# Finer rings for the streamed weights of the token MLP, later ordering of SP's tasks and tighter scheduling margins in a fused attention and MLP kernel

## The chip, the cores and the metric

One core of one Trainium2 chip. The metric is the device time of one execution in microseconds (us), the median of several executions. Spans and granted clocks belong to single executions; the granted TensorE clock was 0.999 to 1.000 in every profiled run here.

## The reference

With x of 2048 tokens by 1024, xn its layer norm, 32 heads, 4 segments of 512 tokens, the kernel computes

```python
xn = layernorm(x)
A: q, k, v = xn@wq, xn@wk, xn@wv              # per segment: causal softmax(q k^T) v, gated with a
   o = g * (phi(q) M) / (phi(q) z) + (1-g) * softmax(..) v   # memory M, z summed over earlier segments
   A = o @ wo
B: h = layernorm(xn)
   u = gelu(h^T-mixed: einsum('sd,sf->df', h, w1) + b1)       # w1: 2048 x 3584, mixes tokens
   B = (einsum('df,fs->ds', u, w2) + b2)^T                    # w2: 3584 x 2048
out = x + A + B
```

The first 215 us are the first MLP product. After that TensorE alternates between attention and the "dense" second product: 32 groups (16 token blocks by two halves), each the sum over 28 row blocks of w2 (for most groups plus 8 matmuls of `o @ wo`). Dense groups fill the time in which attention waits for ACT, POOL or DVE. w2 isn't resident; it is streamed through small rings.

## The kernel before

A Python scheduler inside the kernel keeps a model of every engine's time and decides in which order instructions are written. All DMAs are issued by SP, in program order; a DMA whose wait isn't met holds up all behind it (in the profile before, SP's queue spends 337 us waiting for PE).

```python
class _Ring:                                   # pieces of w2
    def ensure(self, b):
        target = min(b + self.depth, len(self.srcs) - 1)
        while self.issued <= target:           # load piece b+depth when piece b is first used
            k = self.issued
            src, dst = self.srcs[k], self.slots[k % self.n]
            self.fw.dma(dst[:, 0:src.shape[1], :], src, writes=[self.res[k % self.n]])
            self.issued += 1
# ...
class _Flow:
    MARGIN = 120          # a PE task is taken when its inputs are ready this many ns (by the model) ago
    MARGIN_STEP = 110
    PART = 160
    def next(self):                            # which waiting ACT/DVE/POOL/SP task is written next
        # ...
            for e, (fn, ns, busy) in t.engs.items():
                s = max(r, fw.now[e])
                key = (s, t.prio, t.n, s + ns)
# ...
        self.w2r = [e.take(f"w2n{i}", [P, 6, P], BF16) for i in range(4)]   # ring N: 4 pieces of 6
        self.w2l = [e.take(f"w2l{i}", [P, 6, P], BF16) for i in range(3)]   # ring L: 3 pieces of 6
# ...
        self.L = _Stream(k, self, long, "L", k.w2l, k.R_w2l, 2, [3])        # depth 2
        self.N = _Stream(k, self, rest, "N", k.w2r, k.R_w2, 3, [0, 1, 2])   # depth 3
# ... the end of tail(): last projection, by pieces of the last four token blocks
                fw.op("dve", lambda e: e.tensor_tensor(dst, self.ps[:, b, c0:c1], dst, op=ALU.add), ...)
                fw.dma(self.out_d[:, 4 * s + i, h * 512 + c0:h * 512 + c1], dst, ..., is_output=True)
```

The softmax here doesn't subtract the row's maximum and nothing guards it: scores larger than these inputs give would overflow.

Of the kernel before, what the change touches and what calls it, by code (L numbers as in the profile page):

```python
# [6 lines left out]
ACT = mybir.ActivationFunctionType  # L7
ALU = mybir.AluOpType
BF16 = mybir.dt.bfloat16
# [9 lines left out]
P = 128  # L19
# [346 lines left out]
class _Flow:  # L366


    LOOK = 5
    MARGIN = 120  # L370
    MARGIN_STEP = 110
    PART = 160

    def __init__(self, fw, R_bank, free, fill):
        self.fw, self.R_bank, self.free, self.fill = fw, R_bank, free, fill
# [59 lines left out]
    def next(self):  # L435
        fw, best = self.fw, None
        for t in self.avail:
            if t.gate is not None and not t.gate():
                continue
            reads = t.reads if t.box is None else t.reads + [self.R_bank[t.box["b"]]]  # L440
            r = fw.ready(reads, t.writes)
            for e, (fn, ns, busy) in t.engs.items():
                s = max(r, fw.now[e])
                key = (s, t.prio, t.n, s + ns)
                if best is None or key < best[0]:
                    best = (key, t, e, reads)
        return best
# [63 lines left out]
    def run(self, goals):  # L511
# [5 lines left out]
        while self.crit:  # L517
# [3 lines left out]
            for t in self.crit[:self.LOOK]:  # L521
                if t.wall and t is not self.crit[0]:
                    break
                if t.left == 0:
                    r = fw.ready(t.reads, t.writes)
                    if len(self.free) >= t.banks and not (t.wall and not fill.ready(t)):
                        bs = sorted(self.bank_t(b) for b in self.free)[:t.banks]
                        r = max([r, bs[-1]] if t.parts is None else [r, bs[3], bs[-1] - self.PART])
                        if r + (self.MARGIN_STEP if t.wall else self.MARGIN) <= now:
                            pick = t  # L530
# [53 lines left out]
class _Kernel:  # L584
# [95 lines left out]
    def over_early(self):  # L680
        fw = self.fw
        e = _Arena(self.nc, self.early_base, self.early_end)
        wait = _after(*self.R_xin, *self.R_xnt)
        self.wv_sb = e.take("wv_sb", [P, N_DCH, D_MODEL], BF16)
        self.wqr = [e.take(f"wq{i}", [P, N_DCH, P], BF16) for i in range(2)]
        self.wkr = [e.take(f"wk{i}", [P, N_DCH, P], BF16) for i in range(2)]
        self.w2r = [e.take(f"w2n{i}", [P, 6, P], BF16) for i in range(4)]
        self.w2l = [e.take(f"w2l{i}", [P, 6, P], BF16) for i in range(3)]
        self.w2s = [e.take(f"w2s{i}", [P, P], BF16) for i in range(2)]
        self.prod = e.take("prod", [P, 4, P], BF16)  # L690
        self.R_prod = Res("prod", wait)
        self.o_s = [e.take(f"o_s{i}", [P, 4, P], BF16) for i in range(2)]
        self.R_os = [Res(f"o_s{i}", wait) for i in range(2)]
        self.R_wv = [Res(f"wv{i}", wait) for i in range(2)]
        self.R_wq = [Res(f"wq{i}", wait) for i in range(2)]
        self.R_wk = [Res(f"wk{i}", wait) for i in range(2)]
        self.R_w2 = [Res(f"w2n{i}", wait) for i in range(4)]
        self.R_w2l = [Res(f"w2l{i}", wait) for i in range(3)]
        self.R_w2s = [Res(f"w2s{i}", wait) for i in range(2)]
        self.pkT = e.take("pkT", [P, SEG_L], BF16)  # L700
        self.etmp = e.take("etmp", [P, SEG_L], BF16)
        self.R_pkT = Res("pkT", wait)
        self.R_etmp = Res("etmp", wait)
        self.wq_ring = _Ring(fw, [t[:] for t in self.wqr], self.R_wq)
        self.wk_ring = _Ring(fw, [t[:] for t in self.wkr], self.R_wk)
        for i in range(N_UNIT):
            g = i % N_GRP
            self.wq_ring.srcs.append(self.A_wq[:, g * P:(g + 1) * P].rearrange("(dc p) j -> p dc j", p=P))
            self.wk_ring.srcs.append(self.A_wk[:, g * P:(g + 1) * P].rearrange("(dc p) j -> p dc j", p=P))
        self.fill = _Fill(self)  # L710
        self.wq_ring.ensure(0)
        self.wk_ring.ensure(0)
        for bv in range(2):
            fw.dma(self.wv_sb[:, :, bv * 512:(bv + 1) * 512],
                   self.A_wv[:, bv * 512:(bv + 1) * 512].rearrange("(dc p) j -> p dc j", p=P), writes=[self.R_wv[bv]])
# [311 lines left out]
        return self.flow.pe(mms, [R_w] + self.R_xnT[4 * s:4 * s + 4])[0]  # L1027

    def evac(self, dst, R_dst, box, view=lambda x: x):
        self.flow.op({"act": (lambda e, b: e.activation(dst, view(self.bank(b)), ACT.Copy), 600, 540),  # L1030
                      "dve": (lambda e, b: e.tensor_copy(dst, view(self.bank(b))), 690, 727)},  # L1031
                     [], [R_dst], box=box, give=True, prio=0)

# [68 lines left out]
    def step(self, items):  # L1102
        fl = self.flow
        slots, jobs, reads = [], [], []
        for r, blocks in items:
            slot = self.slots.popleft()
            slots.append(slot)
            col, masks = 0, []
            for u, kb in blocks:
                self.slot_of[u, r, kb] = (slot, col)  # L1110
                jobs.append((len(slots) - 1, u, r, kb, col))
                masks.append(col // P)
                col += SEG_L - kb * P
                for R in (self.R_kT[u % 3], self.R_qT[u % 3]):
                    if R not in reads:
                        reads.append(R)
            self.users[slot] = {u for u, _ in blocks}
            items[len(slots) - 1] = (r, blocks, slot, masks)

        n = fl.stage - 1  # L1120
        rs = (3 - n) % 4
        fill = self.fill

        def mms(bs, some):
            for i, u, r, kb, col in some:
                self.fw.mm(self.ps[:, bs[i], col:col + SEG_L - kb * P],
                           self.kT[u % 3][32 * r:32 * r + 32, kb * P:(kb + 1) * P],
                           self.qT[u % 3][32 * r:32 * r + 32, kb * P:SEG_L],
                           start=True, stop=True, tile_position=(32 * r, 0))

        def second(bs, some):
            if n >= fill.PLAIN and fill.L.sliced():
                fill.L.cut(rs)
            mms(bs, some)

        def parts(bs):
            k = min(4, len(bs))
            one = sorted([j for j in jobs if j[0] < k], key=lambda j: j[4])
            two = sorted([j for j in jobs if j[0] >= k], key=lambda j: j[4])
            r1 = [R for R in reads if R is not None]  # L1140
            res = [(lambda: mms(bs, one), r1, bs[:k], 330)]
            if two:
                res.append((lambda: second(bs, two), r1 + (fill.L.slice_reads() if n >= fill.PLAIN else []), bs[k:], 307))
            return res

        box = fl.pe(None, reads, banks=len(slots), wall=True, parts=parts)
        pT, R = self.pT, self.R_pT
        for i, (r, blocks, slot, masks) in enumerate(items):
            fl.op({"act": (lambda e, b, slot=slot: e.activation(pT[:, slot, :], self.bank(b), ACT.Exp, scale=SCALE),  # L1149
                           620, 488)}, [], [R[slot]], box=box[i], give=True)  # L1150
            v = pT[:, slot, :].rearrange("p (j q) -> p j q", q=P)
            if len(masks) > 1:
                ap, pat = v[:, masks[0]:masks[1] + 1:masks[1] - masks[0], :], [[0, 2], [1, P]]
            else:
                ap, pat = v[:, masks[0], :], [[1, P]]
            ns = 180 + 115 * len(masks)
            fl.op({"pool": (lambda e, ap=ap, pat=pat: e.affine_select(ap, ap, pattern=pat, compare_op=ALU.is_ge,  # L1157
                                                                      fill=0.0, base=0, channel_multiplier=-1),
                            ns, ns + 30)}, [R[slot]], [R[slot]])
# [99 lines left out]
    def attention_and_out(self):  # L1259
        fw = self.fw  # L1260
# [15 lines left out]
        steps = self.logit_steps()  # L1276
# [27 lines left out]
                    break  # L1304
        goals = [0, 0]
        knots = [(0, 0)] + [(last[8 * s + 7] + 2, 216 + 285 * s) for s in range(3)]
        knots += [(len(steps) - 1, self.fill.total - self.RESERVE), (len(steps), self.fill.total - 3)]
        for i in range(1, len(steps) + 1):
            (x0, y0), (x1, y1) = next((k0, k1) for k0, k1 in zip(knots, knots[1:]) if k0[0] <= i <= k1[0])
            goals.append(y0 + (y1 - y0) * (i - x0) / (x1 - x0))  # L1310
# [162 lines left out]
class _Fill:  # L1473
# [4 lines left out]
    def __init__(self, k):  # L1478
        self.k = k
        self.closed = []  # L1480
        rest = [(c, half, False, 0) for c in range(12, 16) for half in range(2)]
        long = []
        for j in range(3):
            g = [(c, half, True) for c in range(4 * j, 4 * j + 4) for half in range(2)]
            long += [x + (1,) for x in g[:3]]
            rest += [x + (0,) for x in g[3:]]
        long[-1] = long[-1][:3] + (0,)
        self.L = _Stream(k, self, long, "L", k.w2l, k.R_w2l, 2, [3])
        self.N = _Stream(k, self, rest, "N", k.w2r, k.R_w2, 3, [0, 1, 2])
        self.streams = [self.L, self.N]  # L1490
        self.total = self.L.total() + self.N.total()

# [107 lines left out]
```

## Time and profile before

| | before |
|---|---|
| median of 3 | 692.19 us (691.87 to 692.76) |
| span of the profiled execution | 690.2 us |
| PE busy / weight loads busy | 680.5 / 328.6 us |
| PE idle in waits (drawn) | 3.1 us: 1.3 start, 1.1 fixed gaps, 0.4 w2n, 0.3 mask |
| w2n loads, w2l loads | 115, 45 |
| long transposing issues on SP (over 1.4 us) | 4 of 56 after 200 us |

```profile
q8 instruction: 38, 0.62, 0.4%
q14 instruction: 16, 0.13, 0.1%
```

### The profile page before, as it was taken

The page shows a single profiled execution, that of the slowest core. Times are in us where ns is not written, and L with a number is a line of the kernel's source. Part 1 is how long each engine was busy: PE and PEld are TensorE (multiplying, and loading weights), DVE is VectorE, ACT ScalarE, POOL GpSimd, SP SyncE. Part 2 cuts the span into 40 slices and gives each one's busy share as a digit, 9 for nine tenths or more (in the row PEclk, how much of TensorE's full clock was granted, in tenths as well). Part 3 has the DMA queues.
Part 4 walks back from the last instruction along what each step waited for, and adds up shares of the span by engine and source line. Part 5 has one row for each costly group of instructions (what it writes and reads, how often), then busy time and mean ns, then how long its engine had stood idle before and what let it go on. Part 6 is the DMA issues. An engine that isn't in the chain of part 4 may idle for free.

```text
span 690.2 us, 11956 instructions
## 1 busy us (share of the span) xinstructions
PE 680.5 (99%) x4765; PEld 328.6 (48%) x4846; DVE 226.8 (33%) x500; ACT 313.5 (45%) x616; POOL 153.2 (22%) x379
## 2 busy tenths in 40 slices
PE   9999999999999999999999999999999999999998
PEld 3444444444444544544454444544545544454544
DVE  6731100000002323333453461633534534341524
ACT  7431111111136566564655462735754643644540
POOL 5820000000001233223223131312331331312330
PEclk9999999999999999999999999999999999999999
DMA  8367666325026558766556556465565456446334
GB/s 307 121 183 181 154 156 211 91 61 145 1 103 154 133 135 167 142 142 154 132 121 145 123 123 150 103 151 121 126 149 114 104 119 159 106 111 127 86 85 137
DMA packets 274960, 92.03 MB, mean 133 GB/s; under 512 B 233434, under 2 KB 271322, under 8 KB 274906
## 3 DMA queue, kind: packets, MB, share of 16 engines
q1 hardware_dynamic: 274906, 91.28, 54.1%
q8 instruction: 38, 0.62, 0.4%
q14 instruction: 16, 0.13, 0.1%
HBM read 74.47 MB, written 5.24 MB: 115 GB/s over the span
## 4 chain that ended last, share of the span: by engine, by line
PE 96%; issue 1%; ACT 1%; DMA 1%; POOL 0%; DVE 0%; SPq 0%; POOLq 0%; DVEq 0%
PE ps_all L217 96%; DMA xin<-in_A_x_dram 0%; DMA w2n<-in_B_w_dram 0%; ACT xn_tmp L851 0%; ACT xn_tmp L849 0%; POOL pT L1157 0%; DVE h L890 0%; POOL ln_r L882 0%; ACT pT L1149 0%; SPq L247 0%; DVE qT L1031 0%; POOLq L580 0%; DVE fin L1343 0%; POOL ln_t L880 0%; POOL ln_t L877 0%
## 5 line engine op out<-in xcount | busy, mean ns | idle before, releaser
L1157 POOL TENSOR_SCALAR_AFFINE_SELECT pT<-pT 128x256 bf16<-128x256 bf16 (+1 forms) x320 | 127.0, 405 | 506.8 <-ACT pT L1149 497.1
L217 PE MATMUL ps_all<-h,w1all 128*128 128x512 bf16 x878 | 192.9, 379 | 1.1
L1149 ACT ACTIVATE pT<-ps_all 128x512 bf16<-128x512 f32 x320 | 162.1, 620 | 48.9 <-PE ps_all L217 48.9
L217 PE MATMUL ps_all<-gT,w2n 128*128 128x512 bf16 x618 | 146.8, 379 | 2.2 <-issue 0.5
L217 PEld LDWEIGHTS ps_all<-h,w1all 128*128 128x128 bf16 x896 | 87.5, 98 | 106.3 <-DVE h L890 0.6
L1004 ACT ACTIVATE gT<-ps_all,bc 128x512 bf16<-128x512 f32 x56 | 37.7, 689 | 140.3 <-PE ps_all L217 134.8
L217 PEld LDWEIGHTS ps_all<-gT,w2n 128*128 128x128 bf16 x644 | 60.0, 98 | 69.6 <-issue 2.9
L1200 ACT ACTIVATE ost<-ps_all 128x264 bf16<-128x264 f32 (+1 forms) x99 | 35.0, 375 | 81.8 <-PE ps_all L217 81.0
L217 PE MATMUL ps_all<-xnT,wk 128*128 128x512 bf16 x255 | 60.4, 379 | 0.1
L1463 DVE SCALAR_TENSOR_TENSOR stg<-ps_all,bc,stg 128x512 bf16<-128x512 f32 x32 | 23.9, 747 | 110.7 <-PE ps_all L217 110.6
L217 PE MATMUL ps_all<-wv_sb,xnT 128*128 128x512 bf16 x254 | 59.9, 379 | 0.1
L217 PE MATMUL ps_all<-xnT,wq 128*128 128x512 bf16 x248 | 58.9, 379 | 0.4
L217 PE MATMUL ps_all<-gT,w2l 128*128 128x512 bf16 x226 | 57.8, 380 | 1.1 <-issue 0.5
L217 PEld LDWEIGHTS ps_all<-vA,pT 128*128 128x128 bf16 x1280 | 44.3, 96 | 14.2 <-POOL pT L1157 0.8
L1030 ACT ACTIVATE kT<-ps_all 128x512 bf16<-128x512 f32 x32 | 19.1, 597 | 60.6 <-PE ps_all L217 60.5
L217 PE MATMUL ps_all<-vA,pT 128*128 128x33 bf16 x1280 | 45.0, 177 | 0.5 <-POOL pT L1157 0.3
L217 PEld LDWEIGHTS ps_all<-wv_sb,xnT 128*128 128x128 bf16 x256 | 25.1, 98 | 30.2
L217 PEld LDWEIGHTS ps_all<-xnT,wk 128*128 128x128 bf16 x256 | 25.1, 98 | 30.2
L942 DVE TENSOR_SCALAR gcol<-gcol 128x32 f32<-128x32 f32 x1 | 0.2, 181 | 118.6 <-ACT gcol L940 118.6
L217 PEld LDWEIGHTS ps_all<-xnT,wq 128*128 128x128 bf16 x256 | 24.8, 98 | 29.0 <-issue 0.3
L217 PEld LDWEIGHTS ps_all<-gT,w2l 128*128 128x128 bf16 x244 | 21.3, 98 | 25.1 <-issue 5.8
L1015 DVE TENSOR_SCALAR etmp<-etmp 128x512 bf16<-128x512 bf16 x48 | 14.1, 293 | 55.1 <-ACT etmp L1014 55.1
(74 smaller groups left out, 489.2 us busy)
## 6 DMA issues: line engine op xcount, KB each, us to landing
w2n<-in_B_w_dram SPq DMA_DIRECT2D x92, 192.0 KB, 2.8
w1all<-in_B_w_dram SPq DMA_DIRECT2D x12, 1024.0 KB, 5.3
wq<-in_A_wq_dram SPq DMA_DIRECT2D x32, 256.0 KB, 2.8
wk<-in_A_wk_dram SPq DMA_DIRECT2D x32, 256.0 KB, 3.2
w2l<-in_B_w_dram SPq DMA_DIRECT2D x36, 192.0 KB, 2.9
stg<-in_A_x_dram SPq DMA_DIRECT2D x32, 128.0 KB, 3.3
out_dram<-stg SPq DMA_DIRECT2D x32, 128.0 KB, 2.0
w2n<-in_B_w_dram SPq DMA_DIRECT2D x23, 128.0 KB, 2.5
```

Source lines behind the costliest of these rows:

```text
L217: ins = self.nc.tensor.matmul(out, *args, **kwargs)
L942: fw.op("dve", lambda e: e.tensor_scalar(self.gcol[:], self.gcol[:], 1.0, None, op0=ALU.add), reads=[self.R_gcol], writes=[self.R_gcol])
L1004: fw.op("act", lambda e: e.activation(self.gT[:, fc, half * 512:(half + 1) * 512], self.bank(b), ACT.Gelu_apprx_tanh, bias=self.b1c[:, fc: ...
L1015: fl.op({"dve": (lambda e: e.tensor_scalar(et[:], et[:], 1.0, None, op0=ALU.min), 294, 330)}, [R_et], [R_et], prio=2)
L1030: self.flow.op({"act": (lambda e, b: e.activation(dst, view(self.bank(b)), ACT.Copy), 600, 540), "dve": (lambda e, b: e.tensor_copy(dst, v ...
L1149: fl.op({"act": (lambda e, b, slot=slot: e.activation(pT[:, slot, :], self.bank(b), ACT.Exp, scale=SCALE), 620, 488)}, [], [R[slot]], box= ...
L1157: fl.op({"pool": (lambda e, ap=ap, pat=pat: e.affine_select(ap, ap, pattern=pat, compare_op=ALU.is_ge, fill=0.0, base=0, channel_multiplie ...
L1200: "act": (lambda e, b: e.activation(dst, self.ps[:, b, 0:n * VW], ACT.Copy), 175 + n * 27, 140 + n * 27)},
L1463: engs={"dve": (lambda e, b: e.scalar_tensor_tensor(dst, k.bank(b), k.b2c[:, c:c + 1], dst, op0=ALU.add, op1=ALU.add), 750, 785)},
```

## The change

The intent: shorter pieces with more of them ahead, so that a w2 load is never late; transposing DMAs (pk and o) written later in SP's program, so that they don't block ring loads; tighter margins with corrected durations; more dense work held back for the end, where the last attention steps have nothing else to hide behind.

```diff
-    MARGIN = 120
+    MARGIN = 80
+    SPM = 300
-    PART = 160
+    PART = 200
@@ _Flow.next
-                s = max(r, fw.now[e])
+                s = max(r + (self.SPM if e == "sp" else 0), fw.now[e])
@@ over_early (and R_w2, R_w2l likewise)
-        self.w2r = [e.take(f"w2n{i}", [P, 6, P], BF16) for i in range(4)]
-        self.w2l = [e.take(f"w2l{i}", [P, 6, P], BF16) for i in range(3)]
+        self.w2r = [e.take(f"w2n{i}", [P, 5, P], BF16) for i in range(5)]
+        self.w2l = [e.take(f"w2l{i}", [P, 4, P], BF16) for i in range(4)]
@@ estimates: copies, exp, masks
-  ... ACT.Copy), 600, 540)          +  ... ACT.Copy), 585, 540)
-  ... 620, 488)}                    +  ... 575, 488)}
-            ns = 180 + 115 * len(masks)
+            ns = 225 + 115 * len(masks)
@@ attention_and_out
-        knots += [(len(steps) - 1, self.fill.total - self.RESERVE), ...   # RESERVE = 60
+        knots += [(len(steps) - 1, self.fill.total - 70), ...
@@ _Fill.__init__ : a no-op here, n = 0
+        n = (12 - self.PLAIN) // 4
-        self.L = _Stream(k, self, long, "L", k.w2l, k.R_w2l, 2, [3])
-        self.N = _Stream(k, self, rest, "N", k.w2r, k.R_w2, 3, [0, 1, 2])
+        self.L = _Stream(k, self, long, "L", k.w2l, k.R_w2l, 3, [3])
+        self.N = _Stream(k, self, rest, "N", k.w2r, k.R_w2, 4, [0, 1, 2])
```

More of the change, by code (lines that the diff above doesn't have):

```diff
@@ L696, in over_early @@
         self.R_wk = [Res(f"wk{i}", wait) for i in range(2)]
-        self.R_w2 = [Res(f"w2n{i}", wait) for i in range(4)]
-        self.R_w2l = [Res(f"w2l{i}", wait) for i in range(3)]
+        self.R_w2 = [Res(f"w2n{i}", wait) for i in range(5)]
+        self.R_w2l = [Res(f"w2l{i}", wait) for i in range(4)]
         self.R_w2s = [Res(f"w2s{i}", wait) for i in range(2)]
@@ L1029, in evac @@
     def evac(self, dst, R_dst, box, view=lambda x: x):
-        self.flow.op({"act": (lambda e, b: e.activation(dst, view(self.bank(b)), ACT.Copy), 600, 540),
+        self.flow.op({"act": (lambda e, b: e.activation(dst, view(self.bank(b)), ACT.Copy), 585, 540),
                       "dve": (lambda e, b: e.tensor_copy(dst, view(self.bank(b))), 690, 727)},
@@ L1149, in step @@
             fl.op({"act": (lambda e, b, slot=slot: e.activation(pT[:, slot, :], self.bank(b), ACT.Exp, scale=SCALE),
-                           620, 488)}, [], [R[slot]], box=box[i], give=True)
+                           575, 488)}, [], [R[slot]], box=box[i], give=True)
             v = pT[:, slot, :].rearrange("p (j q) -> p j q", q=P)
@@ L1306, in attention_and_out @@
         knots = [(0, 0)] + [(last[8 * s + 7] + 2, 216 + 285 * s) for s in range(3)]
-        knots += [(len(steps) - 1, self.fill.total - self.RESERVE), (len(steps), self.fill.total - 3)]
+        knots += [(len(steps) - 1, self.fill.total - 70), (len(steps), self.fill.total - 3)]
         for i in range(1, len(steps) + 1):
@@ L1481, in __init__ @@
         rest = [(c, half, False, 0) for c in range(12, 16) for half in range(2)]
-        long = []
+        n = (12 - self.PLAIN) // 4
+        long, rest = [x[:3] + (1,) for x in rest[:n]], rest[n:]
         for j in range(3):
```

## The prediction

> **What bounds the kernel now.** I read the shares of the engines first, then the list of what TensorE (PE) waited for, then the chain of work that ended last, then the PE and SP timelines around the two places where that chain leaves PE. The page of the kernel before:
>
> ```profile
> PE 680.5 (99%) x4765; PEld 328.6 (48%) x4846; DVE 226.8 (33%) x500; ACT 313.5 (45%) x616; POOL 153.2 (22%) x379
> PE 96%; issue 1%; ACT 1%; DMA 1%; POOL 0%; DVE 0%; SPq 0%; POOLq 0%; DVEq 0%
> ```
>
> PE is busy for 680.5 of 690.2 us, and 96% of the chain lies on it. That alone is weak evidence, because a matmul's bar contains its latency. The spacing decides. In the chain during the dense first half:
>
> ```profile
> 36.41 10.74 PE ps_all L217 x49
> 47.15 0.05 issue
> 47.20 10.74 PE ps_all L217 x49
> ...
> 577.90 0.70 DVE qT L1031
> 578.60 0.69 SPq L247
> 579.33 2.75 DMA w2n<-in_B_w_dram
> ...
> 668.31 1.09 ACT pT L1149 x2
> 669.40 0.06 issue
> 669.46 1.53 POOL pT L1157 x2
> ```
>
> From 36.41 to 47.20 are 10.79 us. The page counts 4846 weight loads but 4765 matmuls, so 81 matmul records are missing; with one of them in this stretch it is 50 matmuls of 512 columns, 215.8 ns each. I set the program's 4846 matmuls against the trace's starts: in the attention half the other kinds are as steady: 25 ns for a 33-column matmul, 57 ns for a 132-column one, and 0.64 us for each of the 46 stretches of 32-row logit matmuls (0.638 to 0.653, one shorter). So PE runs back to back nearly everywhere, and the list of what PE waited for is short:
>
> ```profile
> PE ps_all L217 <- DVE gT L800: 1.3, 1, 1.3
> PE ps_all L217 <- issue: 1.1, 7, 0.2
> PE ps_all L217 <- DMA w2n<-in_B_w_dram: 0.4, 1, 0.4
> PE ps_all L217 <- POOL pT L1157: 0.3, 1, 0.3
> ```
>
> The first row is the start-up, the second is fixed gaps around logit stretches; only the last two are stalls. They are understated: a 512-column matmul is drawn 379 ns long but the next may start after 215.8, so 163 ns of a stall hide under the bar. The w2 stall is 0.38 + 0.16 = 0.54 us, the mask stall 0.32 + 0.15 = 0.48 us (rounding included). **About 1.0 us in 690 is avoidable idle time.** That is the first number of this prediction.
>
> The w2 stall, on the PE and then the SP timeline:
>
> ```profile
> 577.70 4.05 PE L217 MATMUL ps_all<-gT,w2n 128*128 128x512 bf16 x18
> 582.13 0.82 PE L217 MATMUL ps_all<-gT,w2n 128*128 128x512 bf16 x3 [0.38 <-DMA w2n<-in_B_w_dram]
> ...
> 576.99 2.30 SPq L247 DMA_TRANSPOSE xnT<-o_s  x1
> 579.33 1.17 SPq L247 DMA_DIRECT2D w2n<-in_B_w_dram  x2
> ```
>
> A dense group starts at 577.70. Its first piece lets the load of the fourth start, three pieces (18 matmuls, 18 x 0.2158 = 3.88 us) ahead. But SP is inside a transposing DMA until 579.29, 2.30 us long where the median of the 56 in this half is 1.2; the load is issued at 579.33, lands 2.75 us later at 582.08, and PE, through with its 18 matmuls, has to wait. Three more w2n loads were nearly late: matmuls started 47, 59 and 142 ns after their load had landed, as against 46 ns in the stall itself.
>
> **What the Trainium skill says.** "Perfetto Trace Analysis", section Identifying the Most-Contended Engine, calls matmul busy share no good measure of the distance to the roofline; I therefore use spacing, and this trace bears the page out in that 99% busy hides 163 ns per stall. "TensorE: Matmul & The Clock Gate", section Back-to-back issue gap, gives N/2.4 + 2.5 ns, 215.8 for 512 columns: the trace agrees, and the granted clock is 1.000. "DMA: Bandwidth & Descriptors", section Anatomy of one DMA, says DMA engines don't wait on semaphores, the issuing sequencer does before dispatch; so everything behind a waiting transpose on SP waits too, as at 576.99 to 579.33. The same section puts most of a small DMA's cost into a fixed part. The trace agrees:
>
> ```profile
> w2n<-in_B_w_dram SPq DMA_DIRECT2D x92, 192.0 KB, 2.8
> w2l<-in_B_w_dram SPq DMA_DIRECT2D x36, 192.0 KB, 2.9
> w2n<-in_B_w_dram SPq DMA_DIRECT2D x23, 128.0 KB, 2.5
> ```
>
> From 192 to 128 KB a landing shortens by only 0.3 us, so 160 KB should save some 0.15 us.
>
> **The change part by part.** *PE's work.* Both programs hold 4846 matmuls of the same kinds and counts, in 46 logit stretches of the same lengths. The rewritten choice of long groups gives the same list, since its new count is (12 - 12) // 4 = 0. Nothing is removed from PE: 0 us.
>
> *The rings.* w2n goes from 4 pieces of 6 (three ahead: 18 blocks, 3.88 us) to 5 of 5 (four ahead: 20 blocks, 4.32 us). Lead grows by 0.43 us, landing shortens by 0.15, together 0.58 us, against the 0.54 us stall and three close calls. w2l goes from two of 6 ahead to three of 4: 12 blocks both times, and a landing of 2.5 instead of 2.9 us. The price is DMAs: 23 groups x 6 instead of 5 (+23), and L's eight cut groups and one full group need 7 pieces each instead of 5 (+18): 41 more. At SP's 0.37 to 0.6 us per issue that is 15 to 25 us more, spread over 470 us in which SP mostly waits (200 us for PE alone). Off the path, except where one is queued ahead of an urgent load. Gain: 0.4 to 0.54 us.
>
> *Transposes later.* Adding 300 ns to an SP task's start in the scheduler moves all tasks it places on SP (transposes, stores, x and wq/wk loads) behind the ring loads that PE's own progress triggers. I expected this to clear the transposes out of the loads' way; the instruction order does not show it. A w2n load follows a transpose directly in 29 cases after, 21 before; such a load with no wait of its own, so held by the transpose alone, 5 after, 6 before. The case at 577 still has the transpose right in front of the load. 0 us by itself; the ring must absorb it.
>
> *Margins.* MARGIN 120 to 80, PART 160 to 200, exp estimated at 575 instead of 620, copies at 585 instead of 600, masks 45 higher. Where PE waits for ACT, the tightest matmuls start 148, 232 and 247 ns after the semaphore; about 47 ns is what a stalled one shows. So 100 ns are spare once and 180 elsewhere, of which 40 + 15 to 45 are spent (exp and mask estimates cancel for the weighted sums). A few gaps of tens of ns: +0 to 0.3 us.
>
> *More kept for the end.* The reserve grows from 60 to 70 (70 x 0.2158 = 15.1 us). But the mask stall at 671 sits between the last logits and the first weighted sum, and in the new order that place holds 12 dense matmuls as before, with ACT's and POOL's last instructions in the same order. The stall of 0.48 us stays. The additional blocks come after the last sums (2 + 8 rather than 3 before the final projection), where the trace shows no wait. 0 us. One load of w2l, needed right after those 12 blocks, is now triggered only when they start: 12 x 0.216 = 2.6 us for 0.4 issue + 2.5 landing; up to 0.3 us, partly under the mask stall.
>
> Sum: -0.5 for the w2 stall, +0.1 for margins, 0 to +0.1 for the end: **about -0.4, or 691.7 us** from 692.19.
>
> **The rivals.** *New stalls outweigh the old.* 41 more SP issues and less slack could make loads or sums late: ten stalls of 0.2 us would give 694. For it: SP order is fragile, one slow transpose issue cost 0.54 us. Against: every w2n load has 0.43 us more lead, and ten stalls would mean that the scheduler's estimates were far off, which the 148 ns say they aren't. *Both stalls go:* 692.19 - 1.02 = 691.2. For it: the intent. Against: the same 12 blocks at the end. *A large gain,* more than 5 us, has nothing to feed on: it would need fewer or shorter matmuls, and there are none. *Transposes too late:* o or pk landing late would idle PE at a weighted sum or at the final projection; the tightest such landing at the projection was 2.0 us early, so 0.3 us later is harmless.
>
> **Range and chances.** Three runs of before span 691.87 to 692.76, so a median can be off by 0.4. Floor: 691.2 - 0.4 = 690.8. Top: no gain, a few new stalls of 0.5 us in all, and noise: 693.0. A 2% change is 13.8 us; only a serial wait repeated in many of the 46 steps could do it. 1% slower, 1% faster (for what I have overlooked), 98% same.
>
> **What would show it.** Right: the wait of PE for a w2n load gone or under 0.1 us, PE's mask wait of about 0.3 us still before the last weighted sums, PE busy 680 to 681 us, 138 w2n loads of which 115 have 160 KB. Wrong: rows of ACT, DVE or a transpose among PE's waits, or the last matmul later than 688 us, or a w2l load awaited at the end.

## The result, and the profile after

The changed kernel took 692.70 us (692.21 to 693.01, 6 runs), the kernel before 692.03 us (691.76 to 692.76, 6 runs). The ratio is 1.0008, 95% interval 0.9995 to 1.0021: the same.

The list of what PE waited for, after:

```profile
PE ps_all L217 <- DVE gT L801: 1.3, 1, 1.3
PE ps_all L217 <- DVE h L891: 0.7, 2, 0.5
PE ps_all L217 <- POOL pT L1158: 0.3, 1, 0.3
```

The w2n row is gone, the mask row has kept its size (line numbers shift by one). The other 0.7 us is the start-up, before 12 us. At the place of the old stall, PE's timeline and then SP's:

```profile
577.63 6.21 PE L217 MATMUL ps_all<-gT,w2n 128*128 128x512 bf16 x28
```

```profile
576.78 1.19 SPq L247 DMA_TRANSPOSE xnT<-o_s  x1
578.02 1.25 SPq L247 DMA_DIRECT2D w2n<-in_B_w_dram  x2
```

28 matmuls without a gap. The transpose still stands directly ahead of the load, but took 1.19 us here, not 2.30. One w2n stall is there all the same, too short to be drawn as a wait: at 415.26 us a matmul that waits for its load starts 0.28 us later than the spacing allows. The mask stall on PE's timeline:

```profile
666.47 2.76 PE L217 MATMUL ps_all<-gT,w2l 128*128 128x512 bf16 x12
669.56 0.27 PE L217 MATMUL ps_all<-vA,pT 128*128 128x33 bf16 x4 [0.33 <-POOL pT L1158]
```

So PE's stream is a little shorter: first `h` matmul to last matmul is 6.56 to 687.56 = 681.00 us before and 6.38 to 687.32 = 680.94 after, and PE ended 0.24 us earlier. Yet the span is 0.4 us longer, 690.6 against 690.2. The loss lies behind the last matmul. The DMA view of the last microseconds, before (687 to 690.3 us) and then after (687 to 690.7); of the issues the last column is from issue to landing:

```profile
q1 hardware_dynamic: 432, 0.26, 24.9%
...
out_dram<-fin SPq DMA_DIRECT2D x1, 80.0 KB, 1.6
out_dram<-fin SPq DMA_DIRECT2D x1, 48.0 KB, 1.5
```

```profile
q14 instruction: 1, 0.01, 1.0%
...
out_dram<-fin SPq DMA_DIRECT2D x1, 80.0 KB, 1.6
out_dram<-fin SPq DMA_DIRECT2D x1, 48.0 KB, 2.0
```

The last store landed 2.0 us after its issue instead of 1.5. In the trace 15 of its 16 completion counts arrive by 689.72 us and the last one at 690.14. It was also issued 0.18 us after the DVE addition it waits for, where before it was 0.03. And there is one packet on the instruction queue, which carries program code, that the kernel before doesn't have there; the page counts 17 on q14 instead of 16. From the start of the last matmul to the end of the span it takes 3.30 us instead of 2.69. That is 0.62 us more and not 0.66 (0.51 of landing and 0.15 of issue), because after its last issue SP runs 20 semaphore waits, which end 1.57 us after the issue even without the fetch: they hid the landing after 1.49 us, but not the one after 2.00.

### The profile page after: what moved, and what is told of

The parts are those of the page before. It is cut to its first block, busy times and chain, and to the rows that moved or that the text cites. A ratio compares the mean times of both kernels' runs of the same rounds, so it can differ in the third digit from the quotient of the medians. Undisturbed runs are those within 1.5% of the kernel's fastest.

```text
span 690.6 us, 12076 instructions
## 1 busy us (share of the span) xinstructions
PE 685.1 (99%) x4846; PEld 327.2 (47%) x4846; DVE 229.5 (33%) x504; ACT 310.6 (45%) x612; POOL 153.5 (22%) x379
## 4 chain that ended last, share of the span: by engine, by line
PE 97%; ACT 1%; DMA 1%; POOL 0%; DVE 0%; issue 0%; POOLq 0%; SPq 0%; DVEq 0%
PE ps_all L217 97%; ACT xn_tmp L850 0%; DMA w2n<-in_B_w_dram 0%; DMA xin<-in_A_x_dram 0%; ACT xn_tmp L852 0%; POOL pT L1158 0%; DVE h L891 0%; ACT pT L1150 0%; POOL ln_r L883 0%; POOLq L581 0%; SPq L247 0%; DVE fin L1344 0%; POOL ln_t L881 0%; DVE ln_mv L866 0%; DVEq L65 0%
## 5 line engine op out<-in xcount | busy, mean ns | idle before, releaser
L217 PE MATMUL ps_all<-gT,w2n 128*128 128x512 bf16 x644 | 150.7, 379 | 0.1
L217 PE MATMUL ps_all<-gT,w2l 128*128 128x512 bf16 x244 | 64.2, 380 | 0.0
L217 PE MATMUL ps_all<-xnT,wq 128*128 128x512 bf16 x256 | 60.5, 379 | 0.0
```

The costliest lines, as they stand in the source:

```text
L217: ins = self.nc.tensor.matmul(out, *args, **kwargs)
```

## The experiments

**What had to be told apart.** Theory F: the 41 additional DMAs make SP's program longer, so one more block of code is fetched, and by chance its fetch falls on the last store. Its rivals: the smaller pieces cost time themselves; chance. And for the rings: is the gain the lead of the loads, and how often was the stall there at all?

All kernels gave correct results. "w2n stalls" is the sum of what matmuls that wait for a w2n load start later than the normal spacing, stalls of over 0.1 us alone, in the one profiled execution, so it includes what hides under the drawn bars.

| run | median us (range) | ratio to before (95%) | w2n stalls us | last store, issue to landing |
|---|---|---|---|---|
| first pair, before | 692.03 (691.76 to 692.76) | | 0.54 | 1.49 |
| first pair, after | 692.70 (692.21 to 693.01) | 1.0008 (0.9995 to 1.0021) | 0.28 | 2.00 |
| e1 copy of before | 691.95 (691.59 to 692.87) | 0.9993 (0.9976 to 1.0010) | 0 | 1.50 |
| e2 after again | 692.60 (691.90 to 693.39) | 1.0000 (0.9985 to 1.0016) | 0 | 2.02 |
| e3 rings only | 692.78 (692.27 to 693.26) | 1.0003 (0.9988 to 1.0018) | 0 | 2.03 |
| e4 all but rings | 693.57 (693.28 to 694.80) | 1.0017 (1.0001 to 1.0033) | 2.1 | 1.50 |
| e5 after + 12 tiny loads | 691.90 (691.39 to 692.73) | 0.9996 (0.9984 to 1.0008) | 0 | 1.50 |
| e6 before + 41 tiny loads | 692.66 (692.28 to 692.92) | 1.0005 (0.9994 to 1.0017) | 0.50 | 2.12 |
| e7 late transposes only | 692.36 (691.74 to 693.11) | 1.0001 (0.9989 to 1.0013) | 0.19 | 1.50 |
| e8 margins only | 693.20 (692.83 to 695.48) | 1.0020 (1.0008 to 1.0033) | 1.3 | 1.50 |
| e9 four w2n pieces of five | 697.22 (696.48 to 699.53) | 1.0079 (1.0064 to 1.0093) | 4.4 | 2.13 |
| e10 after + tiny + mask | 691.97 (691.71 to 693.25) | 1.0000 (0.9988 to 1.0013) | 0.72 | 1.50 |
| e11 rings + tiny + mask | 691.59 (691.30 to 692.14) | 0.9991 (0.9979 to 1.0004) | 0.50 | 1.50 |
| e12 reserve only | 692.14 (691.75 to 692.48) | 0.9999 (0.9985 to 1.0013) | 0.50 | 1.49 |

e1 to e4, e5 to e8 and e9 to e12 ran together, each with its own runs of before (medians 692.49, 691.99, 692.23). In the first, one execution of before took 694.47 us and one 693.51, which widens its intervals. By the record's own measure (2%) every kernel here is "same"; by their intervals only e4, e8 and e9 differ from before at all. The smaller differences rest on the traces.

### e1: the kernel before, unchanged

> The kernel before, unchanged but for a comment: it measures what two equal programs differ by. Theory A (the change leaves PE's stream within 0.1 us, and the 0.67 us between the medians came from outside it): ratio 1.000, the interval no wider than 0.0015. The trace shows the same stall of PE for a w2n load at about 582 us (0.38 us drawn) only if the long transposing issue on SP (2.30 us in the first trace) recurs; if it was chance, that row is missing here and the gain of the new rings was never there to be had in most executions.

Measured: ratio 0.9993, as a copy should have, but an interval of 0.0034 in width, wider than I had written. At that place the trace has a w2n stall of 0.09 us only, and none over 0.1 us elsewhere: the transpose at 577.06 us took 1.91 us and the load was nearly in time. So the 0.54 us of the first profile is there in some executions only. **The gain I had counted was the value of one execution.**

### e2: the changed kernel again

> The changed kernel once more. If the 0.67 us is real, the ratio is 1.0005 to 1.0012 again and its interval excludes 1; if it was scatter, 0.9993 to 1.0005. In the trace: last matmul at 687.2 to 687.7 us, PE's mask wait 0.33 us, no wait for w2n above 0.2. The rival that sees the loss in the last store expects that store to land again 2.0 us after its issue, the rival of chance 1.5 us.

The ratio, 1.0000, fits scatter; but the medians of e2 and e1, from the same chip and the same rounds, are again 0.65 us apart. The last store again landed after 2.0 us, with the q14 packet beside it, although PE's last matmul came at 686.86 us, 0.32 us earlier than in e1 (and earlier than the 687.2 I had expected). Times alone could not settle this; the store's landing could.

### e3 and e4: the rings alone, and everything but the rings

```diff
# e3: before, with the six ring lines of the change    # e4: the changed kernel, with those six lines undone
```

> Only the ring sizes of the change (41 more loads). Theory: the w2n stall at 582 us gone, the mask stall of 0.33 us drawn stays; last matmul 0.3 to 0.6 us earlier than in the copy of before; ratio 0.9993 to 1.0003. Rival (the smaller loads themselves cost time, at SP or at the end): ratio 1.0006 or more.

> All of the change without the rings: four pieces of six and three of six as before. Theory: lead of w2n stays 3.88 us, so one to three PE waits for w2n of 0.1 to 0.5 us remain; mask stall stays; ratio 0.9997 to 1.0008. Rival (the rings cost the time): this one is as fast as before or faster, ratio 0.9990 to 1.0000.

e3 has no w2n stall, and 2.03 us at the last store: the end goes with the rings or with something that comes with them. Its last matmul came 0.22 us before e1's, less than I had expected. Its ratio is at the upper edge of what I had written and decides nothing. e4 lands the store after 1.5 us and is nevertheless the slower, because of two long stalls (0.91 us each) and a short one (0.28) on w2n loads; this profile is of the slowest of its five executions:

```profile
PE ps_all L217 <- DMA w2n<-in_B_w_dram: 1.5, 2, 0.8
```

That was neither theory's number (I had allowed stalls of up to 0.5 us): without the rings, the rest of the change makes w2n loads late. Which part does, e7 and e8 tell.

### e5 and e6: moving the fetch, both ways

```diff
# K = 12 in the changed kernel (e5), K = 41 in the kernel before (e6)
+        self.spare = nc.alloc_sbuf_tensor_at("spare", [P, 48], BF16, offset=229248)
+        self.R_spare = Res("spare")
@@ hidden(), the dense first half, where PE doesn't wait for SP
+                if 5 <= n < 5 + K:
+                    fw.dma(self.spare[:, 0:32], self.B_w2[0:P, 32 * n:32 * n + 32], writes=[self.R_spare])
```

> The changed kernel with 12 tiny loads (8 KB each) more on SP during the dense first half. The three traced kernels with the new rings hold one more 8 KB packet on the instruction queue q14 (17 or so instead of 16), fetched at 688.3 to 688.8 us, just as the last store runs; that store lands 2.0 us after its issue, and 1.5 us in the three kernels without the rings. Theory F (the last store waits behind this fetch, which falls there because of how many instructions SP's program holds): 12 more DMAs move the fetch some 12 DMAs earlier, before the last stores, so the last store lands 1.5 us after its issue again, and the median falls 0.4 to 0.7 us below that of the changed kernel, to 691.9 to 692.2. Rival (the rings slow the end in another way, or 2.0 us is chance): landing stays 2.0 us.

> The kernel before with 41 tiny loads more on SP in the dense first half, so that its SP program has as many instructions as that of the changed kernel; rings and order untouched. Theory F: a packet on q14 at 688 to 689 us, the last store issued 0.15 us late and landing 2.0 us after its issue instead of 1.5; span 0.5 to 0.7 us longer, 690.5 to 690.9 if no w2n stall falls in. Rival (it is the new rings): 1.5 us.

Both came out as theory F has it. e5, the DMA view of 687 to 690 us: no instruction packet, and 1.5 us.

```profile
q1 hardware_dynamic: 432, 0.26, 27.4%
...
out_dram<-fin SPq DMA_DIRECT2D x1, 80.0 KB, 1.6
out_dram<-fin SPq DMA_DIRECT2D x1, 48.0 KB, 1.5
```

Its fetch stands at 673.4 us, where nothing depends on it. e6, the kernel before with its own rings and its own order but a longer SP program, 687 to 691.1 us:

```profile
q1 hardware_dynamic: 432, 0.26, 20.1%
q14 instruction: 1, 0.01, 0.5%
...
out_dram<-fin SPq DMA_DIRECT2D x1, 128.0 KB, 1.7
out_dram<-fin SPq DMA_DIRECT2D x1, 80.0 KB, 1.6
out_dram<-fin SPq DMA_DIRECT2D x1, 48.0 KB, 2.1
```

Fifteen completion counts are in by 689.93 us, the sixteenth at 690.48. The 41 loads run 400 us earlier and touch nothing that PE or the rings use, so their number alone moved the end of the traced execution; the medians are 692.66 against 691.99 us. Over all 14 profiles the store landed after 2.0 to 2.1 us in the five kernels that have the fetch there (after, e2, e3, e6, e9) and after 1.5 us in the nine others; from the last matmul's start to the end of the span it is 3.30 to 3.43 us in the five and 2.68 to 2.69 us in the nine. The times by themselves (ratios 0.9996 and 1.0005) aren't clear of noise; the traces are.

### e7 and e8: the later transposes alone, the margins alone

```diff
# e7: before, with                                     # e8: before, with
+    SPM = 300                                         MARGIN 80, PART 200, copies 585,
+ s = max(r + (self.SPM if e == "sp" else 0), ...)     exp 575, masks 225 + 115 n
```

> Only the later ordering of SP's tasks (300 ns). Theory: lead of the w2n loads as before (3.88 us), transposes still directly ahead of some of them; ratio 0.9990 to 1.0010, w2n stalls of 0 to 0.6 us in the trace as before. Rival (this part is what cost all-but-rings its two stalls of 0.9 us): two or more w2n stalls, in sum over 1 us, and a ratio above 1.001.

> Only the margins and the estimates of durations. Theory from the slack in the trace: no wait of PE for ACT, DVE or POOL beside the mask stall, ratio 0.9995 to 1.0010. Rival (the tighter packing of PE's program puts the dense groups where their loads come later, which is the cause of the two stalls of 0.9 us in all-but-rings): w2n stalls over 1 us in sum, ratio above 1.001.

e7: nothing, as expected. e8 is 1.2 us slower, and this is clear of noise. No row of ACT or DVE other than the start-up's appeared among PE's waits, so the slack I had read from the trace was real; the cost came through the w2n loads, two of which are late, by 0.92 and 0.37 us. The larger stall, on PE's timeline and SP's in e8:

```profile
410.06 5.34 PE L217 MATMUL ps_all<-gT,w2n 128*128 128x512 bf16 x24
416.16 1.04 PE L217 MATMUL ps_all<-gT,w2n 128*128 128x512 bf16 x4 [0.75 <-DMA w2n<-in_B_w_dram]
```

```profile
410.21 1.53 SPq L247 DMA_DIRECT2D w2n<-in_B_w_dram  x1
411.78 0.54 SPq L247 DMA_DIRECT2D wq<-in_A_wq_dram  x1
412.37 0.58 SPq L247 DMA_DIRECT2D w2n<-in_B_w_dram  x1
412.99 1.19 SPq L247 DMA_TRANSPOSE xnT<-o_s  x1
```

and SP's in the copy of before, at the same group:

```profile
409.13 1.63 SPq L247 DMA_TRANSPOSE xnT<-o_s  x1
410.81 1.17 SPq L247 DMA_DIRECT2D w2n<-in_B_w_dram  x2
412.02 0.51 SPq L247 DMA_DIRECT2D wq<-in_A_wq_dram  x1
```

The last four matmuls wait for the load issued at 412.37 (they wait for its semaphore), so the transpose at 412.99, written behind it, did not hold up its issue. Counted from the group's first matmul (410.06; in the copy 409.81), this load was issued after 2.31 us instead of 1.62: a wq load now stands before it, and the issue of the w2n load before that took 1.53 us instead of 0.58. It also landed 3.74 us after its issue instead of 2.65. Why it landed so late was not tried; in e9 two w2n loads that were issued directly before such a transpose took 3.8 and 3.6 us.

The smaller stall is a case of a transpose in the way:

```profile
364.63 2.38 SPq L247 DMA_TRANSPOSE xnT<-o_s  x1
367.05 1.13 SPq L247 DMA_DIRECT2D w2n<-in_B_w_dram  x2
```

With the new margins it is written between the group's loads (first matmul at 364.02), directly ahead of the one that the last four matmuls need; in the copy it starts before the group, at 363.38 (first matmul at 364.37). Both long stalls of e4 are of this kind. I had looked for the cost of smaller margins at the wrong engine.

### e9: less lead, the same piece size

```diff
# the changed kernel with
-  [P, 5, P] x 5 slots for w2n, depth 4
+  [P, 5, P] x 4 slots for w2n, depth 3
```

> The changed kernel with four w2n pieces of five instead of five (three ahead: 15 blocks, 3.24 us of lead instead of 4.32). Theory (lead against SP's delay plus 2.7 us of landing decides): w2n stalls return, at several groups, 2 to 6 us of PE idle in sum, ratio 1.003 to 1.009. Rival (piece size, not lead, removed the stall): under 0.5 us of w2n stalls, ratio under 1.002.

```profile
PE ps_all L217 <- DMA w2n<-in_B_w_dram: 3.4, 5, 1.4
```

4.4 us of stalls, and a median 5.0 us over before of the same call (4.6 us over the changed kernel's of e2, from another call). Lead is what counts: with 3.24 us there are stalls at several groups; with 3.88 us four of five profiles with the old margins have 0.19 to 0.54 us of stalls, and the two with the new margins 1.3 and 2.1; with 4.32 us three of six have none, the others 0.28 to 0.72.

### e10, e11 and e12: the end of the last step

```diff
# e10: the changed kernel with the 12 tiny loads and      # e11: before + rings + the 12 tiny loads and
-  ns = 225 + 115 * len(masks)                            -  ns = 180 + 115 * len(masks)
+  ns = 225 + 115 * len(masks)                            +  ns = 180 + 115 * len(masks)
+       + (500 if len(items) == 5 else 0)                 +       + (500 if len(items) == 5 else 0)
# only the last step has 5 items                          # e12: before, with 70 in place of RESERVE = 60
```

> The changed kernel with the 12 tiny loads and with the mask estimate 500 ns higher in the last step, which puts 21 dense matmuls instead of 12 between the last logits and the first weighted sum. Theory: PE's mask wait gone (0.48 us), last store lands 1.5 us after issue, last matmul at 686.4 to 686.9 us; median 691.2 to 691.7, ratio 0.9985 to 0.9995. Rival (the dense work taken from the end opens a wait for the last transposes or for the final projection): a new wait of 0.3 us or more after 675 us, no gain.

> The kernel before with the rings, the 12 tiny loads and the mask estimate 500 ns higher in the last step (17 dense matmuls there), without the change's margins, later transposes and larger reserve. Theory: no w2n stall, no mask stall, last store 1.5 us; median 691.0 to 691.6, at least as fast as the kernel with all parts. Rival: the smaller reserve (4 dense matmuls after the last sums instead of 11) lets PE wait at the final projection, 0.2 us or more.

> Only the reserve, 60 to 70. The same 12 dense matmuls stand before the first weighted sum. Theory: mask stall stays at 0.33 us drawn, nothing gained at the end, ratio 0.9990 to 1.0010. Rival: the mask stall shrinks below 0.1 us.

e12: nothing, and the mask stall kept 0.33 us, as expected. In e10 and e11 the mask stall is gone and nothing new appears after 675 us, but my times were too good: a w2n load was late by 0.72 us in e10's profile, behind a plain wq issue of 1.69 us and a transposing one of 1.27, and by 0.50 in e11's, behind a transposing issue of 3.0 us; in e10 a w2l load was late by 0.29. e11's PE timeline where the mask stall was:

```profile
668.79 2.12 PE L217 MATMUL ps_all<-gT,w2l 128*128 128x512 bf16 x9
670.74 1.89 PE L217 MATMUL ps_all<-wo_sb,oT 128*128 128x512 bf16 x8
672.47 0.26 PE L217 MATMUL ps_all<-vA,pT 128*128 128x33 bf16 x4
```

e11 has the lowest median of all, 691.59 us against 692.23, but its interval contains 1. It is the version I would keep, without a claim that it is faster.

## Why the prediction was right or wrong

The range (690.8 to 693.0) held the measured 692.70, and "within 2%" was right. The point estimate, 0.4 us faster, was not: the medians say 0.67 us slower, a difference that the interval of the ratio doesn't separate from none. That the range held is partly luck: its top left room for new stalls of PE, and the loss came from elsewhere. Step by step:

- **About 1.0 us is avoidable; a large gain has nothing to feed on.** Right as to the large gain; the 1.0 us is that of one execution. In none of the 14 profiles does the stream from the first `h` matmul to the last one take less than 679.9 us; the difference between any two kernels here other than e9 is under 3 us.
- **The rings: gain 0.4 to 0.54 us.** The mechanism was right (e9, e4), the size wrong. The stall in the profiles with the old rings and old margins is 0.54, 0, 0.50, 0.19 and 0.50 us (before, e1, e6, e7, e12), 0.35 on average; with the new ones 0.28, 0, 0, 0, 0.72 and 0.50 (after, e2, e3, e5, e10, e11), 0.25. The average gain seen is 0.1 us, from so few profiles that it isn't distinguishable from none; four of the six with new rings also have the new margins, which cost stalls of their own (e8). I took one execution's stall for the kernel's. The saving in landing was less than the 0.15 us, too: 2.7 us for 160 KB against 2.8 for 192, and the last pieces, 96 KB instead of 128, took 2.7 instead of 2.5; w2l's 2.5 us came out as 2.7.
- **41 more DMAs: off the path.** This is the step that failed. SP's time was indeed free, but the longer program brought one more fetch of code, at the last store. In the profiles the time after the last matmul's start grew by 0.62 us, of which 0.15 is the later issue; that is about the 0.67 us between the medians. e5 takes it away, e6 brings it into the old kernel.
- **Transposes later: 0 us.** Right (e7).
- **Margins: +0 to 0.3 us at ACT's waits.** Wrong in both size and place: alone they cost 1.2 us, through w2n loads that are issued later in their group or take longer to land (e8). With the new rings most of that is absorbed. So the rings' real work in this change seems to have been to pay for the margins: all but the rings is 1.0 us slower than the whole (693.57 against 692.60), although the whole bears the 0.6 us at the end.
- **More kept for the end: 0 us, the mask stall stays.** Right (0.48 us before, 0.49 after; e12). The "up to 0.3 us" for the late w2l load showed as 0.16 us in the first profile.
- **Rival of new stalls outweighing the old.** It was nearest in sign, but named ten stalls of PE; the loss was one event after PE's end.
- **The signs.** Two did not come out as written. PE busy is 685.1 us and not 680 to 681, because this trace holds all 4846 matmul records, where 81 were missing before. And a w2l load was awaited at the end, 0.16 us.
- **Readings of the trace and of a page.** The matmul that started 47 ns after its load had landed (413.61 us) was not nearly but really late, by 0.06 us. The transpose at 576.99 us was not waiting for a semaphore: its input `o_s` was complete at 576.95, and its issue itself took 2.30 us. And the section Back-to-back issue gap of the Trainium skill's "TensorE: Matmul & The Clock Gate" gives N/2.4 + 2.5 ns for an isolated matmul; for a sustained stream of weight loads and matmuls it gives about 131 ns at 512 columns. Here such a stream runs at 215.8 ns, the isolated figure.

Whose code the q14 packet carries, the trace doesn't name, but SP's instruction count tells it. In all 14 profiles q14 packets start when SP has recorded 79 to 82, 207 to 210 and 335 to 338 instructions, steps of 128, and in the eight kernels whose SP has enough of them one more starts at 465 to 474; these packets move with the added DMAs. SP itself pauses there: 0.34 us or more before its 208th, 336th and 464th instruction in every profile, where the instructions next to them can follow within 0.06 us. The last store is SP's 423rd instruction in the kernel before and, with 41 more DMAs, its 464th: hence the 0.15 us of later issue. The tiny loads of e5 make it the 476th. So the place could have been counted before the run.

What stays open: why an issue on SP is sometimes long was not tried. A transposing one takes 1.2 us mostly and 1.4 to 3.0 us in 1 to 6 of 56; of the plain ones after 200 us, 0.37 to 0.43 us in the median, 6 to 14 of about 300 take over 0.7 us. That the packet delays the store's last completion count because both use the same DMA engine is not shown; the trace shows only that they come together.

## What to carry to other kernels

When the busiest engine is already gapless, look at what comes after its last instruction, and compare the landing of the last store between kernels; where DMAs are added, count the instructions of the engine that issues them. Take the size of a rare stall from several executions, not from one. And before changing margins, ask where on the single DMA-issuing queue the long issues and the other loads will then stand.

## What the Trainium skill lacked or had wrong

- "Runtime: NRT & Kernel Launch", section Instruction fetch mechanics, says that code is refilled in blocks of 16 KiB and that the cost of crossing one is mostly hidden. Here the packets on q14 are 8 KB (q8's are 16 KB), and a single one beside the last store of 48 KB put its landing from 1.5 to 2.0 to 2.1 us after issue, and in the changed kernel's profile its issue from 0.03 to 0.18 us after what it waits for.
- "DMA: Bandwidth & Descriptors", section Queues, rings and completion order, names row 14 as the runtime's, refill included, and says that a DMA engine alternates between rows by packets, but not how much a refill packet can cost a kernel's DMA: here 15 of 16 completion counts by 689.72 us, the last at 690.14.
- No page gives the time that issuing a DMA transpose like those here occupies SP ("DMA: Bandwidth & Descriptors" has only sequencer cycles, for other sizes): 1.2 us in most of the 56, up to 3.0 us, against 0.37 us for a plain issue, which can take up to 2.2.
- "DMA: Bandwidth & Descriptors", section Anatomy of one DMA, gives the fixed part of a small DMA for those issued from GpSimd. Here SP issues them, and landings of 2.5 to 2.9 us (medians) for pieces of 96 to 192 KB show that most is fixed there too.
